# A fused sigmoid attention and gated feed-forward kernel: weight conversion moved between stages, raw loads issued later, second-layer operands begun earlier

## The chip, the cores and the metric

The kernel runs on one core of one Trainium2 chip. The metric is the device time of one execution in microseconds; less is better. Three runs of the kernel before took 1148.70, 1149.72 and 1150.18 us; their median, 1149.72 us, is the time before.

## The reference

```python
def _attn_ref(q, k, v):                      # 8 batches, 12 heads, 448 positions, 64 per head, float32
    scores = scale * np.matmul(q, k.transpose(0, 1, 3, 2)) - np.log(S)
    attn = 1.0 / (1.0 + np.exp(-scores))     # a sigmoid, no softmax
    return np.matmul(attn, v).astype(np.float32)

def _moe_ref(x, w_gate, w_val, w_out):       # x 3584x768, weights 768x1536 (twice) and 1536x768
    gate = 1.0 / (1.0 + np.exp(-(x @ w_gate)))
    val = x @ w_val
    return (gate * val @ w_out).astype(np.float32)
...
    x = attn_out.transpose(0, 2, 1, 3).reshape(B * S, H * D)
    return _moe_ref(x=x, **moe_kwargs)
```

The weights come as float64 (each number as two 32-bit words), all else as float32.

## The kernel before, in words

The kernel has three stages that follow each other on TensorE.

**Attention.** 24 head groups `m`, each with 7 beats `g`, give 168 beats. A beat is four score matmuls and four value matmuls in float32 on quarters of the array. ScalarE applies the sigmoid (L503) and copies one accumulator (`x`, L530); VectorE adds the other to it (L537); the sum is stored to `x_dram`. The loop over beats also advances a generator `weights`, which converts weights, and from the eighth head group on the loads, sums and splits of the first pair of batches of x.

**First layer.** A matrix product is done as seven products of block sums (`N_OPS = 7`) in place of eight. A product is nine matmuls in float16: three blocks, each with high and low parts of the weights `A` and of the data `b`, without low times low. Eight visits, numbered 0 to 7, go through four pairs of batches with the gate and value columns of part 0 (groups `jp` 0 to 3) and back through them with part 1 (`jp` 4 and 5). A unit is one column group and one of gate and value: seven products. Two units interleave; `sequence` gives the order, and the visits begin at products 0, 53, 109, 165, 221, 249, 277 and 305 of 336. After a product ScalarE copies its accumulator (L669) or VectorE adds to it (`sum_of`, L636), and ScalarE and VectorE or GpSimd make gate and value of it (L847, L860, L862). During visits 0 to 2 the next pair of batches of x is loaded (L347), summed in magnitude, subtracted on GpSimd (L339) and split into high (ScalarE, L368) and low parts (VectorE, L379, 21 a visit); the splits stand in the visit's products from the 29th on.

**Second layer.** Four visits C with 21 products of 18 matmuls. Their operands `hb` are cast on ScalarE and split on VectorE by the class `Operands` (`chain`); the first of them are made during visit 7.

**Weight conversion** (`convert`, class `Words`) takes a group (one gate or value column group, or one sixth of the output weights) in four chunks of 128x384. A chunk is two steps: the first takes the magnitude and builds sign and exponent (L195, L196), the second the mantissa (L202, L203, L205). Behind a group come a scale (for gate and value weights its maximum is spread over the partitions by a small matmul with `each`, L114 and L621) and seven operands: casts, sums on GpSimd (L253) and low parts on VectorE (`split`, L223), each stored to memory (`send`, L231). `beside(v_, p)` runs so many steps behind product `p` of a visit as the table `due` holds. Twelve groups are gate and value weights, six are output weights. Before the change six groups are converted beside the attention, two in products 2 to 33 of visit 0, and the other ten in `calm`, the 250 products from two into visit 1 to the start of visit 7.

Raw words are loaded by `Words.load` (L179) on the SP queue, which also issues all other transfers in the order of the program: operands `A` (L460), stores of h (L792), stores of converted operands, loads of x. Outside of the attention there are three raw buffers (`AHEAD_FF`), beside it four (`AHEAD`). An instruction of the SP queue that waits holds up all behind it. Each engine works through its own instructions in the order of the program as well.

Of the kernel before, what the change touches and what calls it, by code (L numbers as in the profile page):

```python
# [27 lines left out]
TINY = 2.0 ** -100  # L28
BF16_MAX = 3.3895313892515355e38

BESIDE = 160

AHEAD, AHEAD_FF = 4, 3

FIRST = 6

LAG = 2

# [15 lines left out]
def sigmoid_attention_glu_kernel(ctx: ExitStack, tc: tile.TileContext, qk, v, wg, wv, wo, out):  # L54

    nc = tc.nc
# [11 lines left out]
    KH = NJ // 2  # L68

    N_OPS = 7  # L70
# [11 lines left out]
    h_dram = {}  # L82
# [3 lines left out]
    def chunks(parts, ks):  # L86
        res = []
        for jp, t in parts:
            res += [(wg, wv)[t][2 * jp + j][:, c * CW:(c + 1) * CW] for j in range(2) for c in range(2)]
        for k in ks:  # L90
            res += [wo[k + KH * half][:, c * CW:(c + 1) * CW] for c in range(2) for half in range(2)]
        return res
# [36 lines left out]
    class Scale:  # L129


        def __init__(self, name, n, inv=None):
            self.name = name
            self.sums, self.m, self.s = small(f"{name}c", n), small(f"{name}m"), small(f"{name}s")
            self.inv = small(f"{name}i") if inv is None else inv
# [30 lines left out]
    class Words:  # L166


        def __init__(self, pool, sources, ahead, held, magnitude):
            self.held, self.magnitude = held, magnitude  # L170
            self.pool, self.sources, self.loaded, self.begun = pool, list(sources), [], []
            self.ahead = ahead
            for _ in range(ahead):
                self.load()
# [5 lines left out]
                self.loaded.append(raw.bitcast(U32).rearrange("p (n t) -> p n t", t=2))  # L180

        def begin(self, f):
            raw = self.loaded.pop(0)
            self.magnitude(f, raw[:, :, 1])
            self.begun.append((raw, f))
# [12 lines left out]
        def second(self):  # L198

            raw, f = self.begun.pop(0)  # L200
            m = self.pool.tile([P, CW], U32, tag="wm", name="wm", bufs=1)
            nc.vector.tensor_scalar(out=m, in0=raw[:, :, 1], scalar1=11, scalar2=0x80000000, op0=ALU.logical_shift_left, op1=ALU.bitwise_or)  # L202
            nc.vector.scalar_tensor_tensor(out=m, in0=raw[:, :, 0], scalar=21, in1=m, op0=ALU.logical_shift_right, op1=ALU.bitwise_or)  # L203
            self.load()
            nc.vector.scalar_tensor_tensor(out=f, in0=m, scalar=2.0 ** -31, in1=f, op0=ALU.mult, op1=ALU.mult)  # L205

    def magnitude_vector(to, bits):
# [115 lines left out]
    def convert_steps(n_groups, everywhere, lag):  # L323
        return 8 * n_groups + lag + (TAIL + 4 if everywhere else TAIL)
# [11 lines left out]
    n_a = 2 * len(pairs)  # L336
# [97 lines left out]
    starts = [sequence.index((u, 0)) for u in first_unit] + [len(sequence)]  # L434
# [36 lines left out]
    with tc.manual_schedule(), tc.tile_pool(name="att", bufs=2) as att, tc.tile_pool(name="sc", bufs=2, space=PSUM) as scp, \  # L471
# [80 lines left out]
        def warm_up(n):  # L552

            for _ in range(n):
                sc = scp.tile([P, 2, 512], F32, tag="sc", name="sc")
                for h in range(2):
                    for u in range(2):
                        nc.tensor.matmul(sc[halves[u], h, :S], lhsT=zeros[halves[h], :HP], rhs=zeros[halves[h], :S],
                                         start=True, stop=True)
# [4 lines left out]
        warm_up(2)  # L564
        words = Words(att, chunks(halves_of_jps[:FIRST], ()), AHEAD, 6, magnitude_vector)
        weights = convert(words, halves_of_jps[:FIRST], (), max_abs, scaled_gpsimd, 2, None)
        n_weights, done = convert_steps(FIRST, True, 2), 0

        first_x = 2 * NQ + 1
        tags = itertools.chain(SUMS, (f"xt{i}" for i in range(2 * KC)))  # L570
# [7 lines left out]
        beat = 0  # L578
        for m in range(B * NQ):
            for g in range(7):  # L580
                pending.append((m, g, scores(m, g)))
                if len(pending) > LAG:
                    values(*pending.pop(0))
                if g == 0:
                    load_qk(m + 1)
                if g == LAG:
                    load_v(m + 1)
                finish_stores()
                beat += 1
                while done < n_weights and done * BESIDE < beat * n_weights:  # L590
                    next(weights)
                    done += 1
                finish_adds(1)
                if m == B * NQ - 1 and g == 0:
                    load_operands(RING)
                if m >= first_x and g in (1, 3, 5):
                    next(x_loads, None)
                if m >= first_x + 4 and g in (2, 6):
                    next(x_sums, None)
                if m >= first_x + 7 and (g in (2, 5) or g == 0 and m % 2):  # L600
                    next(splits, None)
# [102 lines left out]
    hs = {}  # L704
# [21 lines left out]
    def hold(pr, jps):  # L726
        kept = {(2 * (jp // KC) + t, 2 * (jp % KC) + j) for jp in jps for t in range(2) for j in range(2)}
        big = {}
        for i in range(4):
            for k in range(KH):  # L730
                at = (i * KH + k) // 2
                if at not in big:
                    big[at] = held(at)
                hs[pr, i, k] = big[at][:, k % 2 * S:k % 2 * S + S]
        return (nc.sync.dma_start(out=hs[pr, i, k], in_=h_dram[pr, i, k]) for i in range(4) for k in range(KH) if (i, k) not in kept)

    oper = [None]
    hb = {}
# [37 lines left out]
    chain = [None]  # L776
# [17 lines left out]
    class Visit:  # L794
# [16 lines left out]
        def tick(self):  # L811
            self.p += 1
            p, left = self.p, self.ticks - self.p
            if p % 2 == 0 and self.early:
                self.early.pop(0)()
            if 2 <= p < 20 and p % 3 != 0 or p >= 20:
                next(self.x_loads, None)
            if p >= 17 and p % 2:
                next(self.x_sums, None)
            if p >= 29:  # L820
                next(self.splits, None)
            if p == N_OPS and self.keep:
                self.moves = hold(self.pr, self.jps)
            if p >= N_OPS:
                next(self.moves, None)
            if self.keep and left < 14:
                chain[0].make(14 - left if left > 3 else 12)
            beside(self.v_, p)

        def end(self):  # L830
# [3 lines left out]
        def begin(self, jp, t):  # L834
            pr, jps = self.pr, self.jps
            if t == 0:
                if self.keep and jp == jps[-1]:
                    before_last()
                if self.v_ == 0:
                    unscale(pr, slice(2 * jp, 2 * jp + 2))  # L840
                elif jp == jps[0]:
                    unscale(pr, slice(2 * jp, 2 * jps[-1] + 2))
            of_unit = [back[pr][:, c:c + 1] for c in (2 * jp, 2 * jp + 1)]

            def gate(i, acc):
                gates[i] = sb(f"g{i}")
                nc.scalar.activation(gates[i], acc, AF.Sigmoid, scale=of_unit[0])  # L847
                if i not in (0, 2):
                    scaled(gates[i], gates[i], of_unit[1])

            def value(i, acc):
                at = 2 * (jp // KC) + i % 2, 2 * (jp % KC) + i // 2
                if self.keep:
                    h = hs[(pr,) + at]
                else:
                    h = gates[i]
                    h_dram[(pr,) + at] = dram.tile([P, S], F32, name=f"h{pr}_{at[0]}_{at[1]}")
                    unsent.append((clock[0] + 4, h_dram[(pr,) + at], h))
                if i in (0, 2):
                    nc.vector.scalar_tensor_tensor(out=h, in0=acc, scalar=of_unit[1], in1=gates[i], op0=ALU.mult, op1=ALU.mult)  # L860
                else:
                    nc.gpsimd.tensor_tensor(out=h, in0=acc, in1=gates[i], op=ALU.mult)  # L862
                c = 4 * at[1] + at[0]
                unsummed.append((clock[0] + 3, h, h_sums[pr][:, c:c + 1]))

            return unit(self.b, gate if t == 0 else value)
# [121 lines left out]

    in_first = 2 * len(JPS_OF_PARTS[0]) - FIRST
    words = Words(conv, chunks(halves_of_jps[FIRST:], range(KH)), AHEAD_FF, 4, magnitude_scalar)  # L990
    weights = convert(words, halves_of_jps[FIRST:], range(KH), sum_abs, scaled, 1, in_first)
    n_first = convert_steps(in_first, True, 1)
    n_all = 8 * (2 * JPS - FIRST - in_first) + convert_steps(KH, False, 1)
    calm = range(starts[1] + 2, starts[n_a - 1])
    due = {}
    for ticks, n in ((range(2, 34), n_first), (calm, n_all)):
        for i, t in enumerate(ticks):
# [6 lines left out]
    def before_last():  # L1004
        assert next(weights, None) is None and not list(weights)
        stage.close()
        stage.enter_context(tc.manual_schedule())
        oper[0] = stage.enter_context(tc.tile_pool(name="oper", bufs=1, reuse_waits="tile"))
# [41 lines left out]
```

## Time and profile before

| | before |
|---|---|
| median of three runs | 1149.72 us (1148.70 to 1150.18) |
| the profiled execution, its own time | 1150.75 us |
| its span | 1148.9 us |
| mean granted TensorE clock | 0.993 |
| TensorE busy | 1126.9 us (98%) |
| VectorE, ScalarE, GpSimd busy | 785.0, 677.0, 485.6 us |
| attention's last value matmuls end at about | 263 us |
| bytes moved | 265.31 MB, mean 231 GB/s |

In the rows that follow PE is TensorE's matmul, PEld its weight load, DVE VectorE, ACT ScalarE, POOL GpSimd, and SPq the SP queue. A row of the timeline begins with start and duration in microseconds; behind the count stands, in brackets, the time for which the engine stood idle before it, and what ended that. A row of stretches gives the busy time of each engine with its count of instructions, then the granted TensorE clock, the share of the DMA engines and GB/s. A row of groups gives line, engine, operation, output and inputs, the count, and behind the bar the busy time and the mean in nanoseconds.

### The profile page before, as it was taken

How to read it: one execution, taken by the hardware profiler on the slowest of the kernel's cores; microseconds unless marked ns; L12 is line 12 of the kernel's file. 1: busy time of each engine (PE TensorE's matmuls, PEld its weight loads, DVE VectorE, ACT ScalarE, POOL GpSimd, SP SyncE). 2: the span in 40 equal slices, each digit the busy share in tenths (PEclk: the TensorE clock that was granted, in tenths of full speed). 3: DMA queues.
4: the chain of work that ended last, by engine and by line, in shares of the span. 5: the costliest groups of instructions: out<-in, count | busy, mean ns of one | idle time of the engine just before them, and what ended most of it. 6: DMA issues, size and time to landing. Idle time of an engine off the chain costs nothing.

```text
span 1148.9 us, 20691 instructions
## 1 busy us (share of the span) xinstructions
PE 1126.9 (98%) x7268; PEld 550.3 (48%) x7268; DVE 785.0 (68%) x1310; ACT 677.0 (59%) x1284; POOL 485.6 (42%) x417
## 2 busy tenths in 40 slices
PE   9999999999899999998899999999999999999998
PEld 3444344444455555554455555555545555555554
DVE  4578998435884579789777767742356777686773
ACT  6777677876675767866666655554355334262340
POOL 0055687901561333364242233311165286482950
PEclk9999999999999999999899999999999999999999
DMA  7789887887887657844566688957556776877644
GB/s 266 225 265 299 313 268 255 291 284 266 272 268 264 210 182 271 289 155 164 161 205 198 195 271 275 324 163 217 187 167 194 239 238 203 268 211 242 200 123 146
DMA packets 174249, 265.31 MB, mean 231 GB/s; under 512 B 49216, under 2 KB 150976, under 8 KB 174144
## 3 DMA queue, kind: packets, MB, share of 16 engines
q1 hardware_dynamic: 174144, 263.98, 71.4%
q8 instruction: 57, 0.93, 0.3%
q14 instruction: 48, 0.39, 0.1%
HBM read 182.48 MB, written 81.43 MB: 230 GB/s over the span
## 4 chain that ended last, share of the span: by engine, by line
PE 83%; DVE 8%; DMA 3%; issue 2%; ACT 2%; POOL 1%; SPq 0%; DVEq 0%; POOLq 0%; ACTq 0%
PE un L653 65%; PE sc L495 9%; PE av L520 9%; DVE whl L223 1%; DVE wm L203 1%; DMA r<-xd 1%; DVE c L636 1%; DVE wm L202 1%; DMA u<-xd 1%; DVE b L379 1%; DMA A<-ad 1%; DMA ad<-whl 1%; DVE wf L205 1%; DMA c<-xd 0%; ACT junk L102 0%
## 5 line engine op out<-in xcount | busy, mean ns | idle before, releaser
L653 PEld LDWEIGHTS <-A 128*128 128x128 f16 x3024 | 296.3, 98 | 280.4 <-issue 7.3
L653 PE MATMUL un<-b,v 128*128 128x448 f16 x1512 | 300.0, 355 | 9.7 <-ACT u L669 7.1
L653 PE MATMUL un<-b,A 128*128 128x448 f16 x1512 | 300.0, 355 | 1.6 <-DVE c L636 1.6
L653 PE MATMUL un<-hh,A 128*128 128x448 f16 x1008 | 273.0, 353 | 0.0
L653 PEld LDWEIGHTS <-v 128*128 128x128 f16 x1512 | 148.4, 98 | 149.9 <-issue 13.8
L503 ACT ACTIVATE a<-sc,bias 128x896 f32<-128x896 f32 x168 | 169.1, 1007 | 64.5 <-PE sc L495 57.0
L653 PE MATMUL un<-hl,A 128*128 128x448 f16 x504 | 177.7, 353 | 0.0
L520 PE MATMUL av<-a,v 64*64 64x448 f32 x1344 | 159.3, 538 | 1.0 <-DVE x L537 1.0
L495 PE MATMUL sc<-qk 64*64 64x448 f32 x1344 | 160.1, 541 | 0.0
L862 POOL TENSOR_TENSOR g<-c,g 128x448 f32<-128x448 f32 x44 | 58.3, 1324 | 200.4 <-DVE c L636 130.8
L189 POOL TENSOR_SCALAR wf<-wf 128x384 f32<-128x384 f32 x72 | 44.8, 622 | 222.0 <-ACT wf L211 154.4
L636 DVE TENSOR_TENSOR c<-un,u 128x448 f32<-128x448 f32 x72 | 44.8, 622 | 80.0 <-PE un L653 73.9
L847 ACT ACTIVATE g<-c,back 128x448 f32<-128x448 f32 x72 | 48.0, 667 | 82.4 <-DVE c L636 76.6
L495 PEld LDWEIGHTS sc<-qk 64*64 64x64 f32 x1344 | 52.6, 134 | 76.7 <-issue 62.0
L253 POOL TENSOR_TENSOR wf<-wf 128x384 f32<-128x384 f32 x72 | 83.9, 1169 | 8.1 <-DVE whl L223 7.3
L520 PEld LDWEIGHTS av<-a,v 64*64 64x64 f32 x1344 | 51.7, 133 | 73.6 <-issue 70.4
L339 POOL TENSOR_TENSOR b<-b 128x448 f32<-128x448 f32 x48 | 67.5, 1441 | 40.6 <-DVE hl L379 40.6
L339 POOL TENSOR_TENSOR v<-v 128x448 f32<-128x448 f32 x48 | 64.0, 1361 | 33.2 <-DVE hl L379 32.1
L537 DVE TENSOR_TENSOR x<-av,x 128x448 f32<-128x448 f32 x48 | 29.8, 620 | 65.9 <-ACT x L530 65.9
L339 POOL TENSOR_TENSOR r<-r 128x448 f32<-128x448 f32 x36 | 46.6, 1300 | 28.3 <-DVE b L379 25.3
L102 ACT ACTIVATE junk<-g 128x448 bf16<-128x448 f32 x88 | 50.6, 574 | 12.7 <-POOL g L862 8.9
L669 ACT COPY p<-un 128x448 f32<-128x448 f32 x48 | 25.3, 526 | 54.1 <-PE un L653 54.0
(348 smaller groups left out, 1350.0 us busy)
## 6 DMA issues: line engine op xcount, KB each, us to landing
A<-ad SPq DMA_DIRECT2D x168, 192.0 KB, 3.5
A<-oo SPq DMA_DIRECT2D x168, 192.0 KB, 2.9
qk<-qk SPq DMA_DIRECT2D x23, 896.0 KB, 5.5
h<-g SPq DMA_DIRECT2D x88, 224.0 KB, 3.6
ad<-whl SPq DMA_DIRECT2D x84, 192.0 KB, 4.3
bd<-b SPq DMA_DIRECT2D x30, 448.0 KB, 4.4
b<-bd SPq DMA_DIRECT2D x30, 448.0 KB, 6.0
v<-vv SPq DMA_DIRECT2D x24, 448.0 KB, 5.0
```

Source lines behind the costliest of these rows:

```text
L102: nc.scalar.activation(junk[:, :x.shape[-1]], x, AF.Abs, accum_out=to)
L189: nc.gpsimd.tensor_scalar(out=f, in0=f, scalar1=F32_MAX, scalar2=F64_ZERO, op0=ALU.min, op1=ALU.max)
L253: nc.gpsimd.tensor_tensor(out=x, in0=y, in1=z, op=op)
L339: engine.tensor_tensor(out=to, in0=x, in1=y, op=ALU.subtract)
L495: nc.tensor.matmul(sc[halves[u], h, :S], lhsT=qkt[halves[h], p, k0:k0 + HP], rhs=qkt[halves[h], p, :S], start=True, stop=True)
L503: nc.scalar.activation(a, sc[:, :, :S], AF.Sigmoid, bias=bias, scale=scale)
L520: nc.tensor.matmul(avs[key][halves[h], :S], lhsT=vt[halves[u], g, h], rhs=a[halves[u], h], start=start, stop=g == last)
L537: nc.vector.tensor_tensor(out=x, in0=other, in1=x, op=ALU.add)
L636: engine.tensor_tensor(out=to, in0=x, in1=y, op=ALU.add)
L653: nc.tensor.matmul(acc, lhsT=w, rhs=m, start=begin and i == 0, stop=i == len(terms) - 1, skip_group_check=not begin)
L847: nc.scalar.activation(gates[i], acc, AF.Sigmoid, scale=of_unit[0])
L862: nc.gpsimd.tensor_tensor(out=h, in0=acc, in1=gates[i], op=ALU.mult)
```

## The change

1. `FIRST` goes from 6 to 7: seven groups are converted beside the attention and one in visit 0. The pace there has two parts: 58 steps over the first 146 beats and the last 17 over the other 22 (before, 67 steps over 160 beats).
2. `calm` leaves out visits 1 and 2 from their 25th product on, where x is split. Its 94 steps then stand in 186 products: 23 in visit 1, 23 in visit 2, 56, 28, 28 and 28 from visit 3 on, to two products into visit 7.
3. A raw load is no longer issued in the second step of the chunk whose buffer it takes, but at the start of the step behind it.
4. In visit 7 the memory of the conversion is given up at its 7th product (before, at the start of group 5), h is loaded with rows 0 and 1 in turn and row 3 ahead of 2, and the operands of the second layer are made from the 9th product on rather than in the last 14.

```diff
-BESIDE = 160
+BESIDE = 146, 168
...
-FIRST = 6
+FIRST = 7
...
         def begin(self, f):
+            while self.spent:
+                self.load()
+                self.spent -= 1
             raw = self.loaded.pop(0)
...
             raw, f = self.begun.pop(0)
+            self.spent += 1
             m = self.pool.tile([P, CW], U32, tag="wm", name="wm", bufs=1)
...
-            self.load()
...
-                while done < n_weights and done * BESIDE < beat * n_weights:
+                while done < n_chunks and done * BESIDE[0] < beat * n_chunks or \
+                        n_chunks <= done < n_weights and (done - n_chunks) * (BESIDE[1] - BESIDE[0]) < (beat - BESIDE[0]) * (n_weights - n_chunks):
...
+        order = [(i, k) for two in ((0, 1), (3, 2)) for k in range(KH) for i in two]
...
-        return (nc.sync.dma_start(out=hs[pr, i, k], in_=h_dram[pr, i, k]) for i in range(4) for k in range(KH) if (i, k) not in kept)
+        return (nc.sync.dma_start(out=hs[pr, i, k], in_=h_dram[pr, i, k]) for i, k in order if (i, k) not in kept)
...
             if p == N_OPS and self.keep:
+                before_last()
                 self.moves = hold(self.pr, self.jps)
...
-            if self.keep and left < 14:
-                chain[0].make(14 - left if left > 3 else 12)
+            if self.keep and p > N_OPS + 1:
+                made = (p - N_OPS) // 2
+                chain[0].make(made if left > 8 else min(made + (9 - left) // 2, 12))
...
-                if self.keep and jp == jps[-1]:
-                    before_last()
...
-    calm = range(starts[1] + 2, starts[n_a - 1])
+    calm = [t for v_ in range(1, n_a - 1) for t in range(starts[v_] + 2, starts[v_] + 25 if v_ < 3 else starts[v_ + 1] + 2)]
```

The order of VectorE's instructions shows what moves. Names are the program's with their buffer numbers: `w31` is the value half of weight group 3, `x1` the second pair of batches, `un` an accumulator of TensorE, `whl` a converted weight operand, `b` an operand of x, `o1` an output-weight group. Line numbers of the changed kernel stand four to six higher.

First, VectorE in visit 0 around the scale of `w31` and of `x1`, before:

```order
L223 SCALAR_TENSOR_TENSOR whl_3673<-wf_3274,w30s_186,whl_3673 128x384
L636 TENSOR_TENSOR c1_3714<-un_3482,p5_3545 128x448
L223 SCALAR_TENSOR_TENSOR whl_3701<-wf_3311,w30s_186,whl_3701 128x384
L124 TENSOR_REDUCE w31m_188<-w31c_187 128x1
L114 TENSOR_SCALAR each_3726<-w31m_188 128x128
L636 TENSOR_TENSOR c0_3759<-un_3533,u2_3593 128x448
L124 TENSOR_REDUCE x1m_226<-x1c_225 128x1
L114 TENSOR_SCALAR each_3765<-x1m_226 128x128
L223 SCALAR_TENSOR_TENSOR whl_3746<-wf_3407,w30s_186,whl_3746 128x384
```

and now:

```order
L641 TENSOR_TENSOR c1_3632<-un_3446,c22_3502 128x448
L124 TENSOR_REDUCE w31m_188<-w31c_187 128x1
L114 TENSOR_SCALAR each_3660<-w31m_188 128x128
L866 SCALAR_TENSOR_TENSOR g2_3520<-un_3404,back0_3312,g2_3520 128x448
L641 TENSOR_TENSOR c0_3695<-un_3683,p1_3571 128x448
L641 TENSOR_TENSOR c1_3732<-un_3560,p5_3610 128x448
L641 TENSOR_TENSOR c0_3771<-un_3598,u2_3652 128x448
L124 TENSOR_REDUCE x1m_226<-x1c_225 128x1
L114 TENSOR_SCALAR each_3777<-x1m_226 128x128
```

The low parts of group `w30` (L223) no longer stand among the evictions (L636, now L641) and the two scales; that group is converted beside the attention.

Second, VectorE in visit 2 among the splits of the last pair of batches, before:

```order
L636 TENSOR_TENSOR c0_6321<-un_6134,u2_6192 128x448
L379 SCALAR_TENSOR_TENSOR b_6310<-r_6113,x3s_235,b_6310 128x448
L223 SCALAR_TENSOR_TENSOR whl_6276<-wf_5301,w50s_198,whl_6276 128x384
L195 TENSOR_SCALAR wf_6202<-wf_6202 128x384
L196 SCALAR_TENSOR_TENSOR wf_6202<-wraw_6033,wf_6202 128x384
L379 SCALAR_TENSOR_TENSOR b_6310<-r_5629,x3s_235,b_6310 128x448
L379 SCALAR_TENSOR_TENSOR b_6354<-r_5664,x3s_235,b_6354 128x448
L223 SCALAR_TENSOR_TENSOR whl_6338<-wf_5419,w50s_198,whl_6338 128x384
L202 TENSOR_SCALAR wm_6374<-wraw_6033 128x384
```

and now:

```order
L641 TENSOR_TENSOR c0_6183<-un_6033,u2_6080 128x448
L383 SCALAR_TENSOR_TENSOR b_6172<-r_6012,x3s_235,b_6172 128x448
L383 SCALAR_TENSOR_TENSOR b_6172<-r_5538,x3s_235,b_6172 128x448
L383 SCALAR_TENSOR_TENSOR b_6205<-r_5558,x3s_235,b_6205 128x448
L641 TENSOR_TENSOR c1_6232<-un_6222,u3_6133 128x448
L866 SCALAR_TENSOR_TENSOR g0_6116<-c1_6232,back2_3314,g0_6116 128x448
L383 SCALAR_TENSOR_TENSOR b_6205<-r_5601,x3s_235,b_6205 128x448
```

Only splits of x (L379, now L383) and evictions are left there.

Third, VectorE in visit 3, before:

```order
L636 TENSOR_TENSOR c0_7444<-un_7284,u2_7325 128x448
L195 TENSOR_SCALAR wf_7391<-wf_7391 128x384
L196 SCALAR_TENSOR_TENSOR wf_7391<-wraw_7233,wf_7391 128x384
L636 TENSOR_TENSOR c1_7496<-un_7486,u3_7382 128x448
L860 SCALAR_TENSOR_TENSOR g0_7367<-c1_7496,back3_3222,g0_7367 128x448
L636 TENSOR_TENSOR c0_7523<-un_7370,u4_7422 128x448
L223 SCALAR_TENSOR_TENSOR whl_7484<-wf_6964,o1s_208,whl_7484 128x384
```

and now, at the same evictions of a unit:

```order
L641 TENSOR_TENSOR c0_7244<-un_7066,u2_7116 128x448
L227 SCALAR_TENSOR_TENSOR whl_7221<-wf_6797,w51s_201,whl_7221 128x384
L207 TENSOR_SCALAR wm_7252<-wraw_7041 128x384
L208 SCALAR_TENSOR_TENSOR wm_7252<-wraw_7041,wm_7252 128x384
L209 SCALAR_TENSOR_TENSOR wf_7123<-wm_7252,wf_7123 128x384
L227 SCALAR_TENSOR_TENSOR whl_7256<-wf_6555,w51s_201,whl_7256 128x384
L199 TENSOR_SCALAR wf_7210<-wf_7210 128x384
L200 SCALAR_TENSOR_TENSOR wf_7210<-wraw_7124,wf_7210 128x384
L641 TENSOR_TENSOR c1_7307<-un_7297,u3_7187 128x448
```

Between two evictions two steps of conversion stand where one stood, and the groups come later: the gate and value weights of group 5 now where output weights stood before.

More of the change, by code (lines that the diff above doesn't have):

```diff
@@ L171, in __init__ @@
             self.pool, self.sources, self.loaded, self.begun = pool, list(sources), [], []
+            self.spent = 0
             self.ahead = ahead
@@ L566, in sigmoid_attention_glu_kernel @@
         weights = convert(words, halves_of_jps[:FIRST], (), max_abs, scaled_gpsimd, 2, None)
-        n_weights, done = convert_steps(FIRST, True, 2), 0
+        n_chunks, n_weights, done = 8 * FIRST + 2, convert_steps(FIRST, True, 2), 0
         first_x = 2 * NQ + 1
```

## The prediction

> **What bounds the kernel now.** I read the page's head and busy rows first, then the table of 25 us stretches for idle TensorE time, then TensorE's timeline at those stretches, and last the chain of waits behind each gap.
>
> ```profile
> span 1148.9 us, 20691 instructions
> PE 1126.9 (98%) x7268; PEld 550.3 (48%) x7268; DVE 785.0 (68%) x1310; ACT 677.0 (59%) x1284; POOL 485.6 (42%) x417
> 312.90 90.23 PE un L653 x477
> ```
>
> TensorE is busy in 98% of the span. In the run of products after 312.90 us one matmul costs 90.23/477 = 0.1892 us, so a first-layer product of nine costs 1.703 us. Nothing in the change touches the number of matmuls; it can only move the places where TensorE waits, or creeps after a wait. Those places, from the timeline of PE (start, duration, what, and in brackets the idle time ahead):
>
> ```profile
> 301.88 1.86 PE L653 MATMUL un<-b,v 128*128 128x448 f16 x9 [1.22 <-DMA h<-g]
> 307.53 0.23 PE L621 MATMUL un<-ident,each 128*128 128x128 bf16 x1 [3.78 <-DVE each L114]
> 307.59 4.68 PE L653 MATMUL un<-b,A 128*128 128x448 f16 x15
> ...
> 525.81 3.29 PE L653 MATMUL un<-b,v 128*128 128x448 f16 x9 [2.59 <-ACT u L669]
> 535.68 3.57 PE L653 MATMUL un<-b,v 128*128 128x448 f16 x18 [1.22 <-ACT c L669]
> 551.40 1.87 PE L653 MATMUL un<-b,v 128*128 128x448 f16 x9
> 557.75 3.52 PE L653 MATMUL un<-b,v 128*128 128x448 f16 x9 [4.49 <-ACT u L669]
> 561.07 6.54 PE L653 MATMUL un<-b,A 128*128 128x448 f16 x27
> ...
> 856.97 1.86 PE L653 MATMUL un<-b,A 128*128 128x448 f16 x9 [1.59 <-DVE c L636]
> ```
>
> Nine matmuls take 1.87 us in the row at 551.40, that is 9 x 0.1892 plus 0.17 for the last to end. After the long gaps they take more: 3.29 and 3.52 us for nine, 6.54 for 27 (5.28 by that rule), 4.68 for 15 (3.01). The granted clock says why (columns: busy us, clock, DMA share, GB/s):
>
> ```profile
> 526.00:530.00 4.00, 4.00 (x14) 0.57 0.34 58
> 558.00:562.00 4.00, 4.00 (x12) 0.50 0.22 82
> ```
>
> So a wait above some 2.5 us is paid a second time. The Trainium skill ("TensorE: Matmul & The Clock Gate", What's actually happening) has the clock fall only after an idle window of about 3.4 us. The trace differs: the gap of 2.59 us was followed by 0.57, so the measurement decides; by the page the 1.42 us behind that gap would be no part of the sum, and the forecast 1.4 us later.
>
> Who made TensorE late? From the chain of waits, in order of time:
>
> ```profile
> 305.67 0.73 DVE whl L223
> 306.50 0.98 DVE each L114
> ...
> 546.92 2.07 DVE b L379 x2
> 550.87 1.25 DVE wm L203
> 552.13 2.90 DMA wraw<-wo
> 557.29 0.42 ACT u L669
> ```
>
> Both long waits end in VectorE's queue. At 307 us a weight group's spread matmul sits in TensorE's queue behind `each`, which stands on VectorE behind two groups' conversion. At 557 us VectorE had the third visit's x split (L379) and a weight conversion (L202 to L223) at once; its late `wm` freed a raw buffer late, the raw load came late, ScalarE waited for it in order, and its copy `u` of the product came last.
>
> **The change, part by part.** *Conversion out of visit 0.* Steps there fall from 34 to 26 in the same 32 products, and only one group's `each` stands there. This removes 1.22 + 3.78 us idle and 4.68 - 3.01 = 1.67 us of low clock: 6.7 us.
>
> *No conversion beside the x splits.* In visit 2, the 31 products after the 25th keep L379 and the evictions alone. This removes 2.59 + 1.22 + 4.49 us idle, and (3.29 - 1.87) + (3.52 - 1.87) + (6.54 - 5.28) = 4.33 us of low clock: 12.6 us. Visit 1 lost nothing and gains nothing.
>
> *Second-layer operands over 22 products.* The wait of 1.59 us at 856.97 stands behind the last operands of the chain in VectorE's queue; spread out, they have 22 x 1.703 = 37 us rather than 14 x 1.703 = 24. The early release of the conversion memory adds no wait, since conversion ends two products into that visit. The other load order only brings h rows 0 and 1 in pairs. Gain 1.6 us; ends 0 and 1.6.
>
> Sum of what can go: 6.7 + 12.6 + 1.6 = 20.9 us.
>
> *The same conversion, denser elsewhere.* The 94 steps that stood in 250 products now stand in 186: 23 in each of visits 1 and 2, 140 in visits 3 to 6. What VectorE has there:
>
> ```profile
> 457.00:557.00 100.00, 91.82 (x476) 46.66 (x475) 85.79 (x141) 68.56 (x167) 45.46 (x41) 0.98 0.59 195
> 600.00:750.00 150.00, 150.00 (x795) 77.55 (x794) 107.57 (x191) 89.57 (x207) 46.99 (x48) 1.00 0.80 250
> ...
> L202 DVE TENSOR_SCALAR wm<-wraw 128x384 uint32<-128x384 uint32 x11 | 9.1, 827 | 0.0
> L196 DVE SCALAR_TENSOR_TENSOR wf<-wraw,wf 128x384 uint32<-128x384 uint32 x12 | 7.6, 630 | 0.4
> L205 DVE SCALAR_TENSOR_TENSOR wf<-wm,wf 128x384 f32<-128x384 uint32 x11 | 7.5, 681 | 0.4
> L636 DVE TENSOR_TENSOR c<-un,u 128x448 f32<-128x448 f32 x12 | 7.5, 623 | 16.3 <-PE un L653 13.7 <-ACT wf L211 2.5
> L195 DVE TENSOR_SCALAR wf<-wf 128x384 uint32<-128x384 uint32 x12 | 7.2, 603 | 0.0
> L203 DVE SCALAR_TENSOR_TENSOR wm<-wraw,wm 128x384 uint32<-128x384 uint32 x11 | 6.7, 608 | 0.4
> L223 DVE SCALAR_TENSOR_TENSOR whl<-wf,o0s,whl 128x384 f16<-128x384 f32 x7 | 6.2, 881 | 0.2 <-ACT whl L368 0.2
> L860 DVE SCALAR_TENSOR_TENSOR g<-un,back,g 128x448 f32<-128x448 f32 x5 | 3.4, 677 | 1.3 <-PE un L653 1.3
> ```
>
> (Third number with a count: VectorE; the groups are those of 575 to 675 us.) VectorE is 107.57/150 = 72% busy at the old pace. Evictions need three L636 and one L860 in seven products, 2.55 of 11.9 us, 21%; the rest, 51%, is conversion and grows by 250/186 = 1.34 to 68%: 89% in all. The stalls of visit 2 came at an average of 86%, but with the splits bunched late. An eviction may be late by about three products (5.1 us, product 3 to product 6 of a unit) before TensorE feels it, and the longest step is L202, L203, L205, L223: 3.0 us. So mostly it fits. What makes it tight is in the spread of single operations (min/median/max):
>
> ```profile
> L195 DVE TENSOR_SCALAR wf<-wf x20: 346/354/1295, 573.8 to 745.3; 128x384 uint32<-128x384 uint32 x20
> L202 DVE TENSOR_SCALAR wm<-wraw x20: 346/366/1296, 579.0 to 749.2; 128x384 uint32<-128x384 uint32 x20
> ```
>
> Some of these take 0.9 us longer than the median; with less idle time beside GpSimd more of them will. Today's excess is (0.603 - 0.354) + (0.827 - 0.366) = 0.71 us a chunk; a third more of it adds about 0.25 us a chunk, at a chunk in four products (94 steps, two a chunk, in 186 products) 0.06 of 1.703 us or 4%, so 93%. I take 2 us of new waits in visits 3 to 6. Bounds: zero below; above, every one at 1.296 us, which adds 2 x 1.296 - 1.43 = 1.16 us a chunk, 0.25 chunks a product over 140 products, 41 us of work, against the 11% left (26 us): 15 us. For the two x spreads that now end their run behind a dense window (visits 1, 2) I take 1 us, ends 0 and 3.8 (the wait for `each` above).
>
> *Seventh group beside the attention.* It adds to VectorE four chunks and seven splits, and here the magnitude and the maximum are VectorE's too:
>
> ```profile
> 200.00:225.00 25.00, 25.00 (x270) 10.06 (x266) 12.71 (x24) 19.99 (x26) 22.88 (x18) 1.00 0.85 293
> 225.00:250.00 25.00, 25.00 (x272) 10.18 (x268) 8.60 (x15) 19.70 (x24) 6.67 (x5) 1.00 0.85 284
> ...
> L208 DVE TENSOR_SCALAR wf<-wraw 128x384 uint32<-128x384 uint32 x11 | 4.8, 440 | 0.0
> L105 DVE TENSOR_REDUCE w11c<-wf 128x1 f32<-128x384 f32 x4 | 2.2, 542 | 0.0
> ```
>
> Per chunk 3.35 + 0.44 + 0.54 = 4.33 us, so 4 x 4.33 + 7 x 0.88 = 23.5 us. From 200 to 250 us VectorE idles 12.3 + 16.4 = 28.7 us and is nearly free after; the steps up to there get sparser (58 in 146 beats, before 50 in 119). It hides; without that cover it costs up to 23.5. On the SP queue it brings four loads of 384 KB and seven stores of 192 KB, 2.9 MB; over the last 70 us that is 41 GB/s beside the 284 to 293 there, and takes the DMA share from 0.85 to about 0.97, with `qk` loads among them that have a head's seven beats (10.5 us) to land. I take 0.5 us for both, since 14 of its casts now fall on GpSimd in the last 25 beats.
>
> *Raw loads one step on.* The load leaves the SP queue's place where it waited for VectorE:
>
> ```profile
> SPq L179 <- DVE wm L203: 178.4, 57, 9.0
> DMA to landing us min/median/max: 3.0/3.5/6.0
> ```
>
> Behind each such wait stood operand loads and h stores. One step is two products, 3.4 us, so most of the wait has passed at issue. The load is then wanted two steps on, 6.8 us, with at most 6.0 us to land; ScalarE waits in order if it does not. Zero, ends -1 and +2.
>
> The profiled execution took 1150.75 us: 1150.75 - 20.9 + 2 + 1 + 0.5 = 1133.4. The median of the runs, 1149.72, stands 1.03 below it: 1132.
>
> **Rivals.** *VectorE becomes the bound in visits 3 to 6.* The Trainium skill ("SBUF — State Buffer", Who interferes with whom) says that VectorE's two-port modes and GpSimd hold a shared port pair as an exclusive lock. By that every added overlap costs a full GpSimd operation, and the 1.296 us rows agree. For: 93% worked out above, against: 600 to 750 us shows no wait at 72%. With 7 to 15 us given back, 1137 to 1147; middle 1141.
>
> *The splits themselves are too much.* If L379 and the evictions alone keep VectorE late in visit 2, the 12.6 us stay: 1145. Against: visit 1 had its splits beside lighter conversion and lost nothing.
>
> *The other side: the seventh group lands on the attention's path.* TensorE's accumulators there wait for VectorE's adds. If VectorE, full up to 192 us, stays full and late to the end, 23.5 us come on top instead of 0.5: 1155. It decides from about 19 us of the 23.5. Against it stand the 28.7 idle us.
>
> **How the numbers follow.** Forecast as told (1126 to 1137): 0.65. Visits 3 to 6 bound: 0.18. Splits too much: 0.06. Attention longer: 0.07, part of it still level. Else 0.04. The range reaches from all 20.9 us gained and a little of the attention's slack, 1126, to the middle of the first rival, 1142. A change under 0.2% cannot be told from none here. Faster 0.90, same 0.04, slower 0.06.
>
> **What would show it.** Right: no gap above 1 us at the places of the timeline rows above, clock 1.00 there; VectorE at 23 of 25 us in visits 3 to 6 with gaps below 1 us; the attention's end within 2 us of before. Wrong: `DVE c` or `ACT u` ahead of TensorE in visits 3 to 6 with the clock below 1; `DVE x` ahead of TensorE after 190 us; a wait of ScalarE for `wraw`.

## The result and the profile after

| | before | after |
|---|---|---|
| median | 1150.18 us (1148.70 to 1152.99, 5 runs) | 1131.34 us (1130.81 to 1132.56, 5 runs) |
| the profiled execution, its span | 1150.75, 1148.9 us | 1132.56, 1130.8 us |
| mean granted TensorE clock | 0.993 | 0.998 |

The ratio after to before is 0.9834 (95% interval 0.9817 to 0.9851), 18.8 us less. The forecast was 1132 us, its range 1126 to 1142. Of the five executions of the kernel after, two had a mean clock of 0.998 and took 1132.51 and 1132.56 us (the latter is the profiled one); the three at 1.000 took 1130.81 to 1131.34.

The page of the kernel after, its head and busy row:

```profile
span 1130.8 us, 20697 instructions
PE 1121.1 (99%) x7269; PEld 556.3 (49%) x7269; DVE 793.1 (70%) x1318; ACT 670.4 (59%) x1265; POOL 495.8 (44%) x424
```

TensorE's work is the same; the span lost what TensorE waited or ran at a low clock. The waits of TensorE that are left after the start (who waited, for whom, total, times, longest), and their places in its timeline:

```profile
PE un L658 <- DVE c L641: 2.9, 1, 2.9
PE un L658 <- DMA v<-ad: 0.6, 1, 0.6
```

```profile
495.35 6.66 PE L658 MATMUL un<-b,A 128*128 128x448 f16 x27 [2.94 <-DVE c L641]
...
669.54 10.38 PE L658 MATMUL un<-b,v 128*128 128x448 f16 x54 [0.57 <-DMA v<-ad]
...
800.95 39.32 PE L658 MATMUL un<-b,A 128*128 128x448 f16 x207
840.11 0.54 PE L658 MATMUL un<-hh,A 128*128 128x448 f16 x2
```

Of the waits shown of before none is left. Visit 0 runs through, the splits of visit 2 run through (the row of 500 to 550 us below: TensorE busy 50.00 of 50), and the last run of the first layer (`un<-b,A`) goes into the second layer (`un<-hh,A`) at 840 us with no gap. Two waits are new: 0.57 us at 669 us, and 2.94 us at 492 us, where conversion ends in visit 2 (products 2 to 24 of visits 1 and 2 are called their dense runs below). The second is followed by low clock: 27 matmuls take 6.66 instead of 5.28 us. Three stretches of after (busy us of PE, PEld, DVE, ACT and POOL, clock, DMA share, GB/s):

```profile
300.00:325.00 25.00, 25.00 (x135) 12.94 (x134) 16.73 (x34) 16.61 (x36) 12.20 (x10) 1.00 0.61 185
...
500.00:550.00 50.00, 50.00 (x266) 25.86 (x265) 28.51 (x45) 31.21 (x65) 11.75 (x9) 1.00 0.32 99
...
600.00:750.00 150.00, 149.32 (x790) 77.02 (x788) 134.50 (x241) 99.30 (x236) 58.82 (x60) 1.00 0.86 271
```

VectorE is 134.50/150 = 90% busy in visits 3 to 6, where it was 72%; 89 to 93% had been worked out.

### The profile page after: what moved, and what is told of

Its sections match the earlier page's. It is cut to its first block, busy times and chain, and to the rows that moved or that the text cites. A ratio compares the mean times of both kernels' runs of the same rounds, so it can differ in the third digit from the quotient of the medians.

```text
span 1130.8 us, 20697 instructions
## 1 busy us (share of the span) xinstructions
PE 1121.1 (99%) x7269; PEld 556.3 (49%) x7269; DVE 793.1 (70%) x1318; ACT 670.4 (59%) x1265; POOL 495.8 (44%) x424
## 4 chain that ended last, share of the span: by engine, by line
PE 91%; DVE 5%; DMA 2%; issue 1%; ACT 1%; SPq 0%; DVEq 0%; ACTq 0%
PE un L658 68%; PE av L524 11%; PE sc L499 11%; DVE whl L227 1%; DMA wraw<-wo 1%; DVE wm L208 1%; DVE c L641 1%; DVE wm L207 1%; DVE wf L199 0%; DVE wf L200 0%; DMA h<-g 0%; DMA A<-ad 0%; DVE wf L209 0%; PE sc L562 0%; DVE g L866 0%
## 5 line engine op out<-in xcount | busy, mean ns | idle before, releaser
L658 PE MATMUL un<-b,v 128*128 128x448 f16 x1512 | 296.3, 353 | 0.7 <-DMA v<-ad 0.6
L499 PE MATMUL sc<-qk 64*64 64x448 f32 x1344 | 166.2, 540 | 0.2 <-ACT a L507 0.2
L524 PE MATMUL av<-a,v 64*64 64x448 f32 x1344 | 165.4, 538 | 0.0
L499 PEld LDWEIGHTS sc<-qk 64*64 64x64 f32 x1344 | 56.4, 134 | 72.8 <-issue 54.5
L641 DVE TENSOR_TENSOR c<-un,u 128x448 f32<-128x448 f32 x72 | 44.7, 621 | 65.2 <-PE un L658 62.3
L524 PEld LDWEIGHTS av<-a,v 64*64 64x64 f32 x1344 | 55.2, 133 | 68.7 <-issue 61.5
L200 DVE SCALAR_TENSOR_TENSOR wf<-wraw,wf 128x384 uint32<-128x384 uint32 x72 | 54.6, 759 | 2.4
```

The lines of the kernel that those rows point to most:

```text
L200: nc.vector.scalar_tensor_tensor(out=e, in0=raw[:, :, 1], scalar=0xC0000000, in1=e, op0=ALU.bitwise_and, op1=ALU.bitwise_or)
L499: nc.tensor.matmul(sc[halves[u], h, :S], lhsT=qkt[halves[h], p, k0:k0 + HP], rhs=qkt[halves[h], p, :S], start=True, stop=True)
L524: nc.tensor.matmul(avs[key][halves[h], :S], lhsT=vt[halves[u], g, h], rhs=a[halves[u], h], start=start, stop=g == last)
L641: engine.tensor_tensor(out=to, in0=x, in1=y, op=ALU.add)
L658: nc.tensor.matmul(acc, lhsT=w, rhs=m, start=begin and i == 0, stop=i == len(terms) - 1, skip_group_check=not begin)
```

## The experiments

All in one table; "less" and "more" are against the kernel before for the parts alone, against the kernel after (1131.34) for the rest. Kernels of different rows may have run on different chips; the ratio to the kernel before on the same chip is the safer figure, and where the two disagree by 1 us or more the text gives both.

| kernel | median us | ratio to before (95%) | |
|---|---|---|---|
| seven groups alone | 1142.37 | 0.9936 (0.9924 to 0.9948) | 7.2 less |
| no conversion beside splits alone | 1146.25 | 0.9975 (0.9962 to 0.9988) | 3.3 less |
| later raw loads alone | 1148.16 | 0.9989 (0.9981 to 0.9998) | 1.4 less |
| second-layer operands alone | 1147.42 | 0.9981 (0.9971 to 0.9991) | 2.1 less |
| after, conversion beside splits again | 1135.43 | 0.9875 (0.9861 to 0.9888) | 4.1 more |
| after, raw loads as before | 1136.43 | 0.9888 (0.9871 to 0.9906) | 5.1 more |
| after, dense runs ended at product 17 | 1138.32 | 0.9902 (0.9889 to 0.9916) | 7.0 more |
| after, dense runs ended at product 8 | 1153.74 | 1.0036 (1.0023 to 1.0050) | 22.4 more |
| after, subtractions of x later | 1129.04 | 0.9822 (0.9809 to 0.9836) | 2.3 less |
| after, visit 1 used throughout | 1131.68 | 0.9852 (0.9837 to 0.9867) | 0.3 more |
| after, both of these | 1134.54 | 0.9872 (0.9858 to 0.9887) | 3.2 more |
| after, attention's steps sooner | 1141.94 | 0.9932 (0.9919 to 0.9944) | 10.6 more |

### Each part alone

The edits are the four numbered parts of the diff, each on the kernel before.

Seven groups:

> Only the first part on the kernel before: seven groups beside the attention, one in visit 0. Stalls theory: the waits of 1.22 and 3.78 us and the 1.67 us of low clock in visit 0 go, the 12.6 us of visit 2 and the 1.6 us ahead of the second layer stay, the attention ends within 1 us of before: 6.7 us less, ratio 0.994. Rival (the seventh group's 23.5 us of VectorE work lands on the attention's path): up to 17 us more, ratio up to 1.015, with TensorE waiting for DVE x after 190 us.

7.2 us less, as the stalls theory had it. TensorE reaches the first layer at 262.14 us (before 262.98), visit 0 has no wait, and visit 2 has all of its own.

No conversion beside the splits:

> Only the second part: no conversion beside the x splits, the same steps denser elsewhere. Stalls theory: 12.6 us of visit 2 go, visit 0's 6.7 us stay, and the dense run of visit 2 gives the 4.3 us back that the changed kernel shows at 492 us: 8 to 9 us less, ratio 0.992 to 0.993. Rival (the wait at 492 us comes of the later raw loads, not of density): 12.6 us less, ratio 0.989, no wait behind visit 2's dense run.

Only 3.3 us less: both theories missed. The waits of visit 2's splits are gone and the one behind its dense run is there (2.95 us at 503 us), but new ones came in visits 3 and 4. Timeline of PE:

```profile
645.65 1.86 PE L653 MATMUL un<-b,v 128*128 128x448 f16 x9 [0.85 <-ACT u L669]
677.12 10.38 PE L653 MATMUL un<-b,v 128*128 128x448 f16 x54 [0.67 <-ACT c L669]
697.57 8.03 PE L653 MATMUL un<-b,v 128*128 128x448 f16 x27 [3.26 <-ACT u L669]
```

The kernel after has the same density there and lost 0.57 us. What differs there is above all the place of the raw loads; they are put back by themselves further below.

Later raw loads:

> Only the third part: the raw load at the start of the step behind. Theory: the SP queue's wait for VectorE's wm falls from 178 us to some 30, and the time stays within 2 us, since the waits of TensorE hang on VectorE's own queue: ratio 0.998 to 1.002. Rival (the SP queue's wait held up operand loads and so made the waits of visit 2): 5 us or more less, ratio below 0.996.

1.4 us less, within the 2 us. The waits of visits 0 and 2 stay as they were. The SP queue's wait for `wm` fell as expected (before 178.4 us, 57 times; here):

```profile
SPq L180 <- DVE wm L208: 30.8, 23, 5.6
```

So the SP queue's long wait was no cause of the waits of visit 2. The longest of them is 4.51 us here; the chain behind it runs through VectorE's splits and evictions to ScalarE's copy and holds no raw load.

Second-layer operands:

> Only the fourth part: the second layer's first operands over 22 products. Theory: the 1.59 us ahead of the second layer go, nothing else moves: 1.6 us less, ratio 0.9986. Rival (the wait stands behind the last eviction whatever the order): no change.

The 1.59 us ahead of the second layer are gone, and 2.1 us less (1.0 to 3.3 by the interval) agrees with 1.6.

The four alone add up to 14.0 us, together they give 18.8. The 4.8 us between (5.4 by the ratios) belong to no part by itself.

### Undone from the kernel after

```diff
-    calm = [t for v_ in range(1, n_a - 1) for t in range(starts[v_] + 2, starts[v_] + 25 if v_ < 3 else starts[v_ + 1] + 2)]
+    calm = range(starts[1] + 2, starts[n_a - 1] + 2)
```

> The changed kernel with its second part undone: conversion again through all products of visits 1 to 6, 252 products for 94 steps, the splits included. Theory: VectorE with splits and conversion together made the waits of visit 2, so 9 to 13 us of waits and low clock return between 480 and 560 us, and the 4.3 us behind the dense run at 492 us and the 0.6 us at 669 us go: 5 to 8 us slower than the changed kernel, 1136 to 1140. Rival (those waits went with the later raw loads): no waits there, 1127.

1135.43 us, 4.1 more. Waits return in the splits of visit 2, and only there: 1.20, 2.94, 0.17, 3.00 and 0.37 us, 7.7 in all; the 0.57 us and the wait at 492 us are gone.

```profile
524.87 3.56 PE L658 MATMUL un<-b,v 128*128 128x448 f16 x18 [2.94 <-ACT c L674]
...
545.44 1.86 PE L658 MATMUL un<-b,v 128*128 128x448 f16 x9 [3.00 <-ACT u L674]
```

This shows the mechanism of the main step: conversion beside the splits makes these waits, with or without the later raw loads. It came out below the lower end of what was expected. In the profiled execution, the shortest of the four (1134.33 us), none of these gaps was followed by low clock (18 and nine matmuls in 3.56 and 1.86 us, full speed).

Raw loads issued as before, in the second step of the chunk:

```diff
         def begin(self, f):
-            while self.spent:
-                self.load()
-                self.spent -= 1
...
             raw, f = self.begun.pop(0)
-            self.spent += 1
...
+            self.load()
```

> The changed kernel with its third part undone: the raw load again in the second step of the chunk. Theory now (the load's place does nothing at the old pace, but at the dense pace the SP queue waits for VectorE's wm in front of operand loads and stores): the waits of 0.85, 0.67 and 3.26 us between 640 and 700 us that the second part showed alone return, with their low clock: 5 to 7 us slower than the changed kernel, 1136 to 1138. Rival (as forecast before: it costs nothing by itself): 1131 within 1.

1136.43 us, 5.1 more (6.2 by the ratios), as the theory had it. TensorE waits 1.18, 0.68, 2.84, 0.52 and 0.87 us in visits 3 to 6 (6.1 in all), each time for ScalarE's copies, and in this execution without low clock behind them; the longest, and the SP queue's wait, which the kernel after has at 26.2 us:

```profile
689.72 5.27 PE L654 MATMUL un<-b,v 128*128 128x448 f16 x27 [2.84 <-ACT u L670]
```

```profile
SPq L179 <- DVE wm L203: 140.3, 54, 7.7
```

A part that is worth 1.4 us at the old pace is worth 5.1 at the dense one. The 3.7 us between (4.9 by the ratios) are most of the 4.8 (5.4) that no part had by itself.

The trace shows the path. ScalarE casts a weight into a buffer `whl`, and can do so only when the store of that buffer's former contents has landed. Its waits for that between 600 and 750 us, first here, then in the kernel after:

```profile
ACT whl L368 <- DMA oo<-whl: 10.9, 4, 4.0
```

```profile
ACT whl L372 <- DMA oo<-whl: 0.3, 1, 0.3
```

And the chain ahead of the wait of 1.18 us, which ends at 638.22 us:

```profile
628.63 1.25 DVE wm L203
629.89 0.33 SPq L179
...
630.79 0.38 SPq L231
...
631.23 4.82 DMA oo<-whl
636.07 0.28 ACT whl L368
```

The raw load (L179) had held the SP queue for 4.6 us until VectorE's `wm` was done. The store of `whl` (L231) stood behind it and landed at 636.05 us; ScalarE, held up for 3.79 us until then, came late to its copy. Ahead of the wait of 2.84 us ScalarE stood 3.95 us for such a store, but there the store itself took 6.5 us to land and the SP queue was not waiting for `wm` just then. So the path is shown link by link for one wait, and for the longest only from the store on.

### How dense it may be

The dense runs of visits 1 and 2 end at product 17 or 8 in place of 25 (`starts[v_] + 17`, `starts[v_] + 8`), so visits 3 to 6 take more of the 94 steps: 0.553 and 0.618 a product in place of 0.505.

> The changed kernel with the dense runs of visits 1 and 2 ended at their 17th product, where GpSimd's subtractions of x begin: 94 steps in 170 products, 0.553 a product. Theory (the wait at 492 us comes of conversion beside those subtractions, VectorE's operations 1.2 to 1.4 us each there): 2.94 + 1.38 us go; VectorE in visits 3 to 6 goes from 90% to 97%, with 0 to 5 us of waits: 1127 to 1132. Rival (it comes of density alone): the wait moves to the end of the shorter run and 1131 or more remain.

> The changed kernel with the dense runs of visits 1 and 2 ended at their 8th product: 94 steps in 152 products, 0.618 a product. By the working of the forecast VectorE then needs 51% x 250/152 + 21% = 105% of visits 3 to 6 (238 us) and some 5% more for overlaps with GpSimd: 12 to 24 us of waits there, less the 4.3 us of visit 2: 1139 to 1151. Rival (VectorE has more room than that, since its idle time is taken up first by contention that goes away): below 1135.

1138.32 and 1153.74 us, both above what was expected. With 17 the wait at 492 us is gone, but visits 3 to 6 hold eight waits, 9.1 us in all, of which two:

```profile
663.62 5.27 PE L658 MATMUL un<-b,v 128*128 128x448 f16 x27 [1.85 <-ACT u L674]
672.56 10.38 PE L658 MATMUL un<-b,v 128*128 128x448 f16 x54 [1.97 <-ACT c L674]
```

With 8 there are fourteen, 19.8 us, and low clock behind some; the longest, with 54 matmuls in 12.34 us (10.38 at full speed):

```profile
679.15 12.34 PE L658 MATMUL un<-b,v 128*128 128x448 f16 x54 [6.27 <-ACT c L674]
```

The same stretch of 150 us in both, first with 17, then with 8:

```profile
600.00:750.00 150.00, 140.73 (x738) 71.91 (x736) 134.49 (x250) 97.47 (x230) 55.82 (x58) 1.00 0.87 273
```

```profile
600.00:750.00 150.00, 133.21 (x669) 66.64 (x667) 130.66 (x239) 92.14 (x221) 55.61 (x58) 0.95 0.83 265
```

Over these 150 us VectorE does not go above 134.5 us at any of the three densities, so 90% is the average at which this mix stops getting denser, not 100%. It is no limit of VectorE at every moment, as 25 us with 17 show, in which TensorE lost nothing:

```profile
595.00:620.00 25.00, 25.00 (x135) 12.95 (x134) 24.01 (x44) 16.64 (x42) 8.87 (x9) 1.00 0.66 215
```

What VectorE stood idle for from 600 to 750 us was mostly ScalarE's casts: 10.1 of its 15.5 idle us in the kernel after, and with 17:

```profile
DVE whl L227 <- ACT whl L372: 11.9, 12, 2.0
```

ScalarE in its turn waited 21.8 us for VectorE's evictions there. Two engines that each work in order hold each other; a limit of VectorE alone is not shown. The changed kernel stands close to that edge: a tenth more density brings 9.1 us of waits, and a fifth costs more than the whole gain. The wait at 492 us is not moved to the end of the shorter run, so that density alone does not make it.

### The new wait, and visit 1

VectorE in the kernel after up to that wait, and GpSimd beside it (start, duration):

```profile
489.39 1.36 DVE L227 SCALAR_TENSOR_TENSOR whl<-wf,w40s,whl 128x384 f16<-128x384 f32 x1
490.67 1.28 DVE L207 TENSOR_SCALAR wm<-wraw 128x384 uint32<-128x384 uint32 x1
491.99 1.37 DVE L208 SCALAR_TENSOR_TENSOR wm<-wraw,wm 128x384 uint32<-128x384 uint32 x1
493.39 1.37 DVE L209 SCALAR_TENSOR_TENSOR wf<-wm,wf 128x384 f32<-128x384 uint32 x1
494.68 0.61 DVE L641 TENSOR_TENSOR c<-un,p 128x448 f32<-128x448 f32 x1
```

```profile
485.30 1.24 POOL L343 TENSOR_TENSOR r<-r 128x448 f32<-128x448 f32 x1
...
488.25 1.13 POOL L343 TENSOR_TENSOR r<-r 128x448 f32<-128x448 f32 x1
...
490.30 4.05 POOL L343 TENSOR_TENSOR r<-r 128x448 f32<-128x448 f32 x3
```

Behind the scale of x, four operations of conversion of 1.28 to 1.37 us stand ahead of the eviction `c`, for which TensorE waits; beside all but the first of them GpSimd runs subtractions of x (beside the first it runs a sum of the conversion, 489.34 to 490.33 us). The subtractions were put behind the dense run in the order of the program:

```diff
-            if p >= 17 and p % 2:
+            if p >= 26:
                 next(self.x_sums, None)
```

> The changed kernel with GpSimd's nine subtractions of x in each of visits 0 to 2 begun at the 26th product, one a product, rather than at the 17th, one in two: behind the dense runs instead of beside their last eight products; nothing else moves. Theory (the wait of 2.94 us at 492 us comes of VectorE's operations that meet these subtractions): that wait and its 1.38 us of low clock go, and no other comes: 3 to 4.5 us faster than the changed kernel, 1127 to 1128.5. Rival (density of the conversion alone): the wait stays, 1131.

```profile
493.12 5.27 PE L658 MATMUL un<-b,A 128*128 128x448 f16 x27 [1.41 <-DVE c L641]
```

1129.04 us, 2.3 less (1.4 by the ratios). The wait falls from 2.94 to 1.41 us and its low clock goes: 2.9 us by the trace. By times alone the two intervals overlap (0.9809 to 0.9836 and 0.9817 to 0.9851); the trace shows the difference at its place. It is the fastest version that was run.

The edit did not take the subtractions away from that place, though. TensorE comes to its 26th product of visit 2 at about 491 us (135 products at 1.703 us from 261.37 us), but GpSimd runs ahead of it, and four of them still run beside the same operations of VectorE:

```profile
486.48 5.04 POOL L343 TENSOR_TENSOR r<-r 128x448 f32<-128x448 f32 x4
```

```profile
487.84 1.49 DVE L227 SCALAR_TENSOR_TENSOR whl<-wf,w40s,whl 128x384 f16<-128x384 f32 x1
489.25 1.28 DVE L207 TENSOR_SCALAR wm<-wraw 128x384 uint32<-128x384 uint32 x1
490.57 1.37 DVE L208 SCALAR_TENSOR_TENSOR wm<-wraw,wm 128x384 uint32<-128x384 uint32 x1
491.98 0.56 DVE L209 SCALAR_TENSOR_TENSOR wf<-wm,wf 128x384 f32<-128x384 uint32 x1
```

Only the last operation, which starts after the subtractions have ended at 491.52 us, is back at 0.56 us. So the wait of 1.41 us that is left cannot be put down to density alone: three operations are as long as before. At the short durations that these operations have elsewhere in these traces (0.60, 0.35, 0.56 and 0.56 us) the four would take 2.07 rather than 5.38 us in the kernel after, 3.3 us less, which by that estimate covers the whole 2.94 us. A kernel with no operation of GpSimd beside the four was not run, so the theory is supported and the size of its share is not shown.

Visit 1 lost nothing before, so its splits were given conversion again, as changed only for visit 2:

```diff
-starts[v_] + 25 if v_ < 3 else
+starts[v_] + 25 if v_ == 2 else
```

> The changed kernel with conversion again in all of visit 1, its splits included, and visit 2 as changed: 94 steps in 219 products, 0.43 a product rather than 0.505. Theory (visit 1 begins its run of conversion without a backlog and bears the splits, only visit 2 does not; waits fall with density): no wait of TensorE above 1 us anywhere in the first layer, 1127 to 1129. Rival (splits beside conversion cost the same in either visit): 5 us or more of waits between 400 and 460 us, 1133 or more.

```profile
433.38 5.27 PE L658 MATMUL un<-b,v 128*128 128x448 f16 x27 [1.11 <-DVE c L641]
...
446.88 1.86 PE L658 MATMUL un<-b,v 128*128 128x448 f16 x9 [3.13 <-ACT u L674]
```

1131.68 us, 0.3 more (2.1 by the ratios): the theory falls. Visits 3 to 6 have no wait at 0.43 steps a product, the one at 497 us is down to 0.67, but visit 1 now waits 4.2 us. With both edits:

> Both of these together: visit 1's products used throughout and the subtractions from the 26th product on. Theory: as either one alone, no waits left in the first layer, 1126 to 1128, the less the lower the density. Rival (in visit 1 the later subtractions now fall among conversion and splits together): waits near 430 us, above 1130.

1134.54 us, 3.2 more (4.4 by the ratios); the waits of visit 1 grow to 0.72 + 1.54 + 3.12 us, which fits the subtractions falling among conversion and splits together. The wait behind visit 2's dense run, 0.67 us with visit 1 alone, is 0.81 us with both, so at this density the later subtractions gain nothing there. That visit 1 ran through before is thus no property of visit 1. Low parts of weights (L227) stand among its splits now, four in 405 to 450 us, where one stood:

```profile
L227 DVE SCALAR_TENSOR_TENSOR whl<-wf,w40s,whl 128x384 f16<-128x384 f32 x4 | 4.0, 1005 | 0.0
```

```profile
L223 DVE SCALAR_TENSOR_TENSOR whl<-wf,w40s,whl 128x384 f16<-128x384 f32 x1 | 0.6, 614 | 0.0
```

The first row is of this kernel, the second of the kernel before. These low parts take 3.4 us more and the pace of the conversion is 14% above the old one. But VectorE in all is busy 39.46 of these 45 us, before 38.84, so the amount of work hardly differs; what makes the waits of visit 1 stays open.

### How near the attention is

`BESIDE = 110, 168`: the 58 chunk steps in 110 beats.

> The changed kernel with the 58 chunk steps of the attention in its first 110 beats rather than 146, 0.53 a beat rather than 0.40; the first layer is untouched. This asks how near the attention is to the rival that was feared (VectorE's late adds hold TensorE). VectorE was 97% busy at 0.42 a beat between 109 and 190 us; a third more of conversion, some 12 us of work in these 50 us, should land on the path: attention's end at 270 to 282 us instead of 262, 1139 to 1151. If the accumulators and the idle time after 165 us absorb it: 1131 to 1133.

```profile
PE av L524 <- DVE x L541: 5.5, 5, 1.9
```

```profile
100.00:150.00 50.00, 46.40 (x470) 20.74 (x463) 48.90 (x100) 32.85 (x40) 37.93 (x34) 1.00 0.87 299
```

1141.94 us, 10.6 more. TensorE's value matmuls wait 5.5 us for VectorE's adds (their weight loads 12.5 us, in part at the same time), VectorE is busy 48.90 of 50 us, and the first layer begins at 271.25 us rather than at 262.06. The feared mechanism exists; at 0.40 steps a beat it does not set in, at 0.53 it does, and what then lands on the path stays there although VectorE idles 29 us between 200 and 250.

## Why the prediction was right, point by point

The span fell by 18.1 us, the sum said 17.4.

- *Visit 0*, 6.7 us: 6.7 by the trace (no wait left), 7.2 us less by the part alone.
- *Splits of visit 2*, 12.6 us: all gone, and 0.64 us of smaller gaps there that the sum had left out. Undoing the part brought 7.7 us of waits back. The 4.33 us of low clock in that term were luck of the execution as much as a price, as the gaps below show. The path told for the 4.49 us, by way of a late raw load, was not needed: with later raw loads alone that wait stayed, 4.51 us, with no raw load in its chain.
- *Second layer*, 1.6 us: gone.
- *Denser conversion in visits 3 to 6*, 2 us: 0.57. The load of 90% was well worked out. What was wrong is the measure set against it: room was counted up to 100%, and the bound of 15 us rested on it. A tenth more density brought 9.1 us of waits while VectorE's average stayed at 90%, so next to no room was left.
- *Spreads behind the dense runs*, 1 us: this is the term that was mis-sized. 2.94 + 1.38 = 4.3 us in the profiled execution, and not at the spread's matmul but at the eviction behind four operations lengthened beside GpSimd. That is above the upper end of 3.8 that was set for it.
- *Raw loads*, 0 with ends of -1 and +2: the step that failed in kind. Alone it gave 1.4; in company it holds 5.1 us, and the forecast of the density came out because of it, which the prediction did not see. "Behind each such wait stood operand loads and h stores" was the sentence to follow to its end; the stores of converted operands stood there as well, and it was on these that ScalarE waited.
- *Seventh group beside the attention*, 0.5 us: 0.9 us less, but the start of the first layer stands anywhere from 260.46 to 262.98 us over all profiles except the one with the attention's steps sooner, the kernel with its fourth part alone (no edit there) at 261.52. This is no effect.

The sum rested on a profiled execution of before at 1150.75 us and meets one of after at 1132.56. By the trace the terms now add up to -20.9 - 0.64 + 4.3 + 0.57 - 0.9 = -17.6 us; 0.5 us of the 18.1 is not assigned. Dense conversion came out 1.4 us below its term and the new wait 3.3 us above its own, and the attention's scatter took part of that back: 1132 against 1131.34 is closer than the terms are; that much of it is luck.

One sign of being wrong did show: ScalarE waited for raw words, 4.4 us in three waits, the longest 2.5 (before, 1.1 us in one). No wait of TensorE above 0.57 us came of it.

Of the rivals, the bound of visits 3 to 6 was the real one and lay a tenth of density away, though as VectorE and ScalarE holding each other. Its range was added up in two ways: 1137 puts the 7 us in place of the 2 us of waits, 1147 puts the 15 on top of them. In place of them throughout it is 1137 to 1145 with the middle of 1141 that was given, so the upper end of the forecast's range, 1142, lies 1 us above that middle. That the splits alone are too much is refuted by the stretch of 500 to 550 us. The attention's rival was told apart by its own kernel.

## What to carry to other kernels

A gap of the busiest engine is worth its idle time at least, and where work beside it makes it, moving that work pays if the place it moves to is under its own limit: measure that limit as the busy share at which a stretch stops getting denser, not as 100%. An edit that does next to nothing alone can be the cover of another; sum the parts alone against the whole before any is dropped. Where one engine's operations lengthen beside another's, as from 0.35 to 1.28 us here, move the bursts apart, and look in the trace whether they did move: the order of the program is not the order in time between engines.

## What the runs showed of the hardware

The same gap of TensorE is paid a second time, by matmuls at a low clock behind it, or not, by chance. Two kernels with the same gap of 2.94 us at the same place, first after, then after with the raw loads as before (27 matmuls at 0.1892 and 0.17 are 5.28 us):

```profile
495.35 6.66 PE L658 MATMUL un<-b,A 128*128 128x448 f16 x27 [2.94 <-DVE c L641]
```

```profile
495.28 5.27 PE L654 MATMUL un<-b,A 128*128 128x448 f16 x27 [2.94 <-DVE c L637]
```

The clock granted after the first:

```profile
496.00:500.00 4.00, 4.00 (x17) 0.72 0.46 155
```

The five executions of the kernel after agree with this: the two at clock 0.998 took some 1.5 us longer than the three at 1.000, and the low clock here cost 1.38 us.

Before, nine matmuls after 2.59 us took 3.29 us; with seven groups alone, after 2.58 us, they took 1.86:

```profile
517.87 1.86 PE L654 MATMUL un<-b,v 128*128 128x448 f16 x9 [2.58 <-ACT u L670]
```

With the dense runs ended at product 8, even a gap of 2.25 us was followed by 6.95 us for 27 matmuls (5.28 at full speed), while that of 3.13 us in visit 1 above was followed by nine in 1.86:

```profile
726.48 6.95 PE L658 MATMUL un<-b,v 128*128 128x448 f16 x27 [2.25 <-ACT u L674]
```

So from 2.25 to 2.95 us it went either way, and the three gaps of 3.00 to 3.13 us were not paid again; the gaps of 3.26 us and more (3.26, 3.78, 4.50, 6.27) were all paid twice, and those of 2.04 us and less never. The Trainium skill ("TensorE: Matmul & The Clock Gate", What's actually happening) says that the window of about 3.4 us runs freely and does not start with the work. That agrees with the pairs above, in which the same gap costs more than itself or not. That a whole window must be idle does not agree: 2.25 us are less than one.
